# Batch 0 by token halves: a first G1 and G2 step before the second half is normalised

## Chip, cores, metric

One core of one Trainium2 chip. The metric is device time in microseconds, from repeated executions.

## The reference, cut to what matters

```python
def _attn_ref(x, state):                      # x: 8 batches, 8 heads, 512 tokens, 64; state: 32 slots
    scores = scale * x @ state^T ; a = softmax(scores)       # per token, over the 32 slots
    xread = a @ state
    ...                                                      # sread: the same from the state's side
    return concatenate([xread, sread], axis=2)
def _moe_ref(x, w_in, w_out):                 # 4352 rows, 512 -> 2048 -> 512
    h = x @ w_in ; g = h * sigmoid(h)
    return g @ w_out
```

The kernel folds `state @ w_in` into one matrix W1 per batch, so that h = a @ W1. For a batch, G1 computes h^T in 16 tiles of 128 features for all 512 tokens (two matmuls of 512 columns each, one SILU), and G2 multiplies each tile g by w_out, for four token tiles `tt` of 128 tokens. The tokens of a batch are also counted in chunks c0 to c3 of 128; SILU is h * sigmoid(h), and aT is the transposed a. Fillers are matmuls on zeros that keep TensorE busy.

## The kernel before: the parts concerned

```python
    for hg in range(2):                                   # x of batch 0, by halves of the heads
        nc.sync.dma_start(
            x_f[0][:, ds(4 * hg, 4), :, :],
            x[0, ds(4 * hg, 4)].rearrange("h (p c) d -> p h c d", p=128, c=4),
        )
    ...
    scores(0, 0)                     # 4 heads, all 512 tokens
    exps(0, 0)
    keep_busy(1, psH, "h1")          # filler matmuls on zeros
    pe_transpose_x(0, 1, 2, new_h, both)
    norm(0, 0)                       # GpSimd
    scores(0, 1, 2)
    exps(0, 1)
    norm(0, 1, ((nc.vector, 0, 4),), 2)
    w1_cols(0, [(0, 128)], (nc.scalar, nc.scalar))
    nc.scalar.activation(warm[:], busy[:, 0:1], func=SILU, bias=0.0)   # loads SILU's table
    load_w_in(1024) ...              # the later weight loads, on GpSimd
    keep_busy(3, psH, "h1")
    pss0 = w1_mms(0, [(128, 384)])
    keep_busy(2, psH, "h1")
    ...                              # 8 transposes of the normed scores, copies to aT
    upto(1)                          # G1 of tile 0 (g1_first)
    upto(2)                          # G1 of tile 1
    for ft in range(12):             # G2 with G1 ahead of it
        upto(min(ft + LEAD0[ft], ready))
        ...
```

The softmax here doesn't subtract the row's maximum and nothing guards it: scores larger than these inputs give would overflow.

## Time and profile before

| | before |
|---|---|
| median of 4 runs | 212.85 us (212.72 to 213.00) |
| span of the profiled run | 210.9 us |
| TensorE in the chain that ends last | 95% |
| first G2 product | 12.23 us |
| G1 of tile 5 | 17.73 us |
| last W1 product of batch 0 | 26.04 us |

The prediction shows the lines for these (it starts from 212.93 us, the median of the three runs that it had). The last three rows are the milestones for reading the change: after the last of them both kernels do the same work in the same order. How busy each engine is in the start-up, in stretches of 2 us (columns: stretch, its length, busy time of TensorE, its weight loads, VectorE, ScalarE, GpSimd, each with its instructions in brackets, then granted clock, DMA share, GB/s):

```profile
8.00:10.00 2.00, 1.80 (x28) 0.80 (x29) 1.90 (x7) 1.97 (x6) 0.93 (x1) 1.00 1.24 193
10.00:12.00 2.00, 1.96 (x23) 1.09 (x16) 1.91 (x7) 1.78 (x6) 2.00 (x4) 1.00 1.29 201
```

### The profile page before, as it was taken

The page shows a single profiled execution, that of the slowest core. Times are in us where ns is not written, and L with a number is a line of the kernel's source. Part 1 is how long each engine was busy: PE and PEld are TensorE (multiplying, and loading weights), DVE is VectorE, ACT ScalarE, POOL GpSimd, SP SyncE. Part 2 cuts the span into 40 slices and gives each one's busy share as a digit, 9 for nine tenths or more (in the row PEclk, how much of TensorE's full clock was granted, in tenths as well). Part 3 has the DMA queues.
Part 4 walks back from the last instruction along what each step waited for, and adds up shares of the span by engine and source line. Part 5 has one row for each costly group of instructions (what it writes and reads, how often), then busy time and mean ns, then how long its engine had stood idle before and what let it go on. Part 6 is the DMA issues. An engine that isn't in the chain of part 4 may idle for free.

```text
span 210.9 us, 3866 instructions
## 1 busy us (share of the span) xinstructions
PE 205.3 (97%) x1575; PEld 96.8 (46%) x1575; DVE 74.0 (35%) x146; ACT 139.2 (66%) x244; POOL 39.5 (19%) x62
## 2 busy tenths in 40 slices
PE   7899999999999999999999999999999999999993
PEld 2444354445444444444444544444444444466653
DVE  3851268567831336115211662043412306100011
ACT  3865677899577867697569855996775166644410
POOL 8681213704220402021201202000200000000000
PEclk9999999999999999999999999999999999999999
DMA  6999999995559475644925528115321111011112
GB/s 205 181 204 206 284 256 354 219 273 194 101 145 259 152 137 119 145 154 114 237 75 173 112 71 193 50 50 102 85 64 46 63 56 53 0 50 50 53 50 99
DMA packets 42929, 28.65 MB, mean 136 GB/s; under 512 B 28064, under 2 KB 37792, under 8 KB 42912
## 3 DMA queue, kind: packets, MB, share of 16 engines
q1 hardware_dynamic: 36720, 20.65, 37.7%
q0 software_dynamic: 5904, 7.64, 17.5%
q8 instruction: 12, 0.20, 0.4%
q10 hardware_dynamic: 288, 0.13, 0.2%
q14 instruction: 5, 0.04, 0.1%
HBM read 17.43 MB, written 8.91 MB: 125 GB/s over the span
## 4 chain that ended last, share of the span: by engine, by line
PE 95%; DMA 2%; DVE 1%; ACT 0%; issue 0%; DVEq 0%
PE o L566 51%; PE h L525 26%; PE ps_w L469 4%; PE h L546 3%; PE o_a L566 3%; DMA x_f<-in_x_dram 2%; PE o_part L588 2%; PE ps_sr L416 1%; PE ps_xt L253 1%; PE ps_sc L306 1%; PE ps_scT L332 1%; PE ps_busy L165 1%; PE ps_at L398 0%; PE h L507 0%; DVE W L159 0%; ACT xT L157 0%
## 5 line engine op out<-in xcount | busy, mean ns | idle before, releaser
L566 PE MATMUL o<-w_out_sb,g 128*128 128x512 bf16 x496 | 131.8, 379 | 0.0
L557 ACT ACTIVATE g<-h 128x512 bf16<-128x512 f32 (+1 forms) x143 | 81.2, 573 | 34.2 <-PE h L525 20.1
L566 PEld LDWEIGHTS <-g 128*128 128x128 bf16 x528 | 50.3, 98 | 59.0 <-issue 3.8
L525 PE MATMUL h<-aT,W 128*128 128x512 bf16 x254 | 74.5, 379 | 0.1
L159 DVE COPY o_sb<-o 128x512 f32<-128x512 f32 x15 | 10.4, 691 | 89.8 <-PE o L566 87.3
L525 PEld LDWEIGHTS <-W 128*128 128x128 bf16 x254 | 24.6, 98 | 30.5 <-issue 1.2
L159 DVE CAST W<-ps_w 128x512 bf16<-128x512 f32 (+2 forms) x36 | 22.2, 659 | 23.2 <-PE ps_w L469 23.2
L157 ACT ACTIVATE W<-ps_w 128x512 bf16<-128x512 f32 (+1 forms) x32 | 16.2, 562 | 11.1 <-PE ps_w L469 11.1
L159 POOL CAST x_nat<-x_f 128x512 bf16<-128x512 f32 x24 | 14.2, 631 | 35.9 <-DMA x_f<-in_x_dram 35.9
L157 ACT ACTIVATE o_sb<-o 128x512 f32<-128x512 f32 x16 | 9.5, 597 | 14.3 <-PE o L566 11.8
L362 POOL TENSOR_TENSOR an<-e,rcn 128x512 bf16<-128x512 bf16 x5 | 7.6, 1518 | 48.9 <-DVE rcn L360 39.3
L469 PE MATMUL ps_w<-w_in_sb,stT 64*32 64x512 bf16 (+2 forms) x264 | 10.1, 373 | 0.0
L566 PE MATMUL o_a<-w_out_sb,g 128*128 128x512 bf16 x32 | 10.0, 379 | 0.0
L546 PE MATMUL h<-xmT,w_in_sb 128*128 128x256 bf16 x64 | 9.6, 273 | 0.0
L546 PEld LDWEIGHTS <-w_in_sb 128*128 128x128 bf16 x64 | 6.3, 98 | 3.9
L165 PE MATMUL ps_busy<-busy 128*128 128x512 bf16 x16 | 5.8, 481 | 1.2 <-DVE warm L172 1.2
L359 DVE TENSOR_REDUCE rs<-e 128x32 f32<-128x1024 bf16 x5 | 6.1, 1211 | 2.1 <-DMA e<-eT 2.1
L346 ACT ACTIVATE eT<-ps_scT 128x512 bf16<-128x512 f32 x10 | 5.4, 594 | 1.6 <-PE ps_scT L332 1.6
L786 ACT ACT_TABLE_LOAD x5 | 6.4, 1283 | 0.1
L382 POOL TENSOR_TENSOR an<-exp_nat,rc 128x512 bf16<-128x512 bf16 x3 | 3.1, 1047 | 13.9 <-DMA x_f<-in_x_dram 8.7
L469 PEld LDWEIGHTS <-stT 64*32 64x32 bf16 x264 | 3.2, 90 | 5.2 <-issue 3.9
L768 ACT ACT_TABLE_LOAD x4 | 5.1, 1283 | 0.1
(76 smaller groups left out, 99.8 us busy)
## 6 DMA issues: line engine op xcount, KB each, us to landing
out_dram<-o_sb SPq DMA_DIRECT2D x33, 256.0 KB, 2.4
x_f<-in_x_dram SPq DMA_DIRECT2D x4, 1024.0 KB, 6.3
x_f<-in_x_dram POOLq DMA_DIRECT2D x2, 1024.0 KB, 12.6
w_in_sb<-in_moe_w_in_dram POOLq DMA_DIRECT2D x3, 512.0 KB, 10.2
x_f<-in_x_dram SPq DMA_DIRECT2D x2, 512.0 KB, 4.7
w_out_sb<-in_moe_w_out_dram POOLq DMA_DIRECT2D x4, 256.0 KB, 11.9
w_out_sb<-in_moe_w_out_dram POOLq DMA_DIRECT2D x2, 512.0 KB, 12.1
x_f<-in_x_dram POOLq DMA_DIRECT2D x2, 512.0 KB, 14.9
```

The source lines that it names most:

```text
L157: nc.scalar.activation(dst, src, func=COPY, bias=0.0)
L159: eng.tensor_copy(dst, src)
L165: nc.tensor.matmul(ps[:], busy[:, 0:128], busy[:], start=True, stop=True, skip_group_check=True)
L346: nc.scalar.activation(t[:, hg], scT_ps[hg][:], func=EXP, bias=0.0, scale=SCALE)
L359: nc.vector.tensor_reduce(rs[:], e2[b][:], axis=AX, op=ADD)
L362: eng.tensor_tensor(a[:, hg], e2[b][:, hg], rc[:, hg].to_broadcast([128, 4, 4, NS]), op=MULT)
L469: nc.tensor.matmul(pss[f, hg][ds(32 * s, 32), 0:n], stT[ds(r, 64), b, h // 2, s % 2, :], w_in_sb[ds(r, 64), h // 2, ds(f, n)], start=True, ...
L525: nc.tensor.matmul(h_ps[k][:], W1[b][:, hg, ds(128 * ft, 128)], aT[b][:, hg, :, :], start=(hg == 0), stop=(hg == 1), skip_group_check=True,)
L546: nc.tensor.matmul(ps[:, 0:256], w_in_sb[:, kt, ds(128 * ft, 128)], xmT[:, :, kt].rearrange("p t n b -> p t (n b)"), start=(kt == 0), stop ...
L557: nc.scalar.activation(g[:, 0:n], ps[:, 0:n], func=SILU, bias=0.0)
L566: nc.tensor.matmul(outs[tt][:], gt[b * NFT + ft][:, ds(128 * tt, 128)], w_out_sb[:, ft, :], start=(ft == 0), stop=(ft == NFT - 1), skip_gr ...
L786: nc.scalar.activation(warm[:], busy[:, 0:1], func=SILU, bias=0.0)
```

## The change

Intent: cut batch 0's attention by tokens instead of by heads. Chunks c0 and c1 (256 tokens, all heads) go through scores, softmax and transposes first; G1 of tiles 0 and 1 on these tokens and four G2 products then run while c2 and c3 are normalised. The core of the diff, with cuts:

```diff
-    for hg in range(2):
+    for half in range(2):
         nc.sync.dma_start(
-            x_f[0][:, ds(4 * hg, 4), :, :],
-            x[0, ds(4 * hg, 4)].rearrange("h (p c) d -> p h c d", p=128, c=4),
+            x_f[0][:, :, ds(2 * half, 2), :],
+            x[0].rearrange("h (p c) d -> p h c d", p=128, c=4)[:, :, ds(2 * half, 2), :],
         )
...
-    keep_busy(7, psH, "h1")
+    keep_busy(6, psH, "h1")
...
+    cast_x(0, nc.vector, 2, 1)
+    cast_x(0, nc.gpsimd, 3, 1)
+    load_w_out(4, 2)
+    load_w_out(6, 2)
+    sum0(0)
...
+    norm0(0, nc.vector)
+    norm0(1, nc.gpsimd)
...
+    turn_a0(0, in_bank("a3"))
+    turn_a0(1, in_bank("o0"))
+    pss0 = w1_mms(0, [(128, 384)], ...)
+    keep_busy(2, psA, "a0")
+    w1_out(0, [(128, 128)], (nc.vector, nc.vector), pss0)
+    g1_part(0, 0, new_h)                 # tile 0, first 256 tokens
+    keep_busy(1, psA, "a0")
+    g1_part(1, 0, new_h)
+    w1_out(0, [(128, 256)], (nc.scalar, nc.scalar), pss0, 128)
+    for c in (2, 3):
+        sum0(c)
+    nc.vector.reciprocal(rc0[:, 2:4], rs0[:, 2:4])
+    norm0(2, nc.vector)
+    norm0(3, nc.gpsimd)
+    load_w_in(1024) ...                  # the later weight loads
+    keep_busy(1, psA, "a0")
+    for ft in (0, 1):
+        for tt in (0, 1):
+            G2(0, tt, ft)
+    turn_a0(2, in_bank("a0"))
+    turn_a0(3, in_bank("a3"))
+    g1_part(2, 0, in_bank("a1"))
+    g1_part(3, 0, in_bank("a2"))
+    g1_part(0, 1)                        # tile 0, second 256 tokens
+    g1_part(1, 1)
...
+    for tt in (2, 3):
+        G2(0, tt, 0)
+    for tt in (2, 3):
+        G2(0, tt, 1)
+    pss = w1_mms(0, [(512, 512)])
```

More of the change, by code (lines that the diff above doesn't have):

```diff
@@ L195 @@
     load_w_in(512)
-    load_w_out(4, 4)
     both = (nc.vector, nc.scalar)
@@ L258, in pe_transpose_x @@
             copy(engs[u], xT[b][:, ds(m * u, m), ds(2 * hg, 2), :], ps[:])
-    cast_x(0, nc.vector, 0, 2, 0, 4)
-    cast_x(0, nc.scalar, 2, 2, 0, 4)
     for u in range(2):
@@ L269 @@
     new_o = lambda sh, dt, nm: psO.tile(sh, dt, tag=o_tags.pop(), name=nm)
-    cast_x(0, nc.scalar, 2, 2, 4, 4)
-    cast_x(0, nc.gpsimd, 0, 1, 4, 4)
-    pe_transpose_x(0, 0, 2, new_o, (nc.vector, nc.vector))
-    cast_x(0, nc.vector, 1, 1, 4, 4)
+    cast_x(0, nc.vector, 0, 1)
+    cast_x(0, nc.scalar, 1, 1)
     st_x = pers.tile([128, 8, B, 4, 2, 2], BF16)
@@ L496, with g1_part @@
     h_ps = {}
-    def g1_first():
-        g = gpool.tile([128, 512], BF16, tag="g", name="g")
-        gt[0] = g
-        pss = []
-        for i in range(2):
-            ps = psH.tile([128, 512], FP32, tag="h1", name="h1")
-            pss.append(ps)
-        for i in range(2):
-            for hg in range(2):
-                nc.tensor.matmul(
-                    pss[i][:, 0:256],
-                    W1[0][:, hg, 0:128],
-                    aT[0][:, hg, ds(2 * i, 2), :],
-                    start=(hg == 0),
-                    stop=(hg == 1),
-                    skip_group_check=True,
-                )
-        for i in range(2):
-            nc.scalar.activation(g[:, ds(256 * i, 256)], pss[i][:, 0:256], func=SILU, bias=0.0)
+    h0_ps = {}
+    def g1_part(k, half, new=None):
+        if half == 0:
+            h0_ps[k] = new([128, 512], FP32, "h1")
+            gt[k] = gpool.tile([128, 512], BF16, tag="g", name="g")
+        cols = ds(256 * half, 256)
+        for hg in range(2):
+            nc.tensor.matmul(
+                h0_ps[k][:, cols],
+                W1[0][:, hg, ds(128 * k, 128)],
+                aT[0][:, hg, ds(2 * half, 2), :],
+                start=(hg == 0),
+                stop=(hg == 1),
+                skip_group_check=True,
+            )
+        nc.scalar.activation(gt[k][:, cols], h0_ps[k][:, cols], func=SILU, bias=0.0)
     def g1_half(k, hg):
@@ L520, in g1_half @@
         if hg == 0:
-            if k == 1:
-                h_ps[k] = psA.tile([128, 512], FP32, tag="a1", name="h1")
-            else:
-                h_ps[k] = (bank if k in IN_BANKS else new_h)([128, 512], FP32, "h1")
+            h_ps[k] = (bank if k in IN_BANKS else new_h)([128, 512], FP32, "h1")
         nc.tensor.matmul(
@@ L536, in emit_G1 @@
         if b < B:
-            if k == 0:
-                g1_first()
-                return
             g1_half(k, 0)
@@ L609, with in_bank @@
     IN_BANKS = (4, 5)
-    new_o = lambda sh, dt, nm: psO.tile(sh, dt, tag=o_tags.pop(), name=nm)
+    def in_bank(tag):
+        return lambda sh, dt, nm: (psO if tag[0] == "o" else psA).tile(sh, dt, tag=tag, name=nm)
+    e0 = pers.tile([128, 4, H, NS], BF16)
+    an0 = pers.tile([128, 4, H, NS], BF16)
+    rs0 = pers.tile([128, 4, H, 1], FP32)
+    rc0 = pers.tile([128, 4, H, 1], FP32)
+    aT[0] = att.tile([128, 2, 4, 128], BF16, tag="aT", name="aT")
+    xT[0] = xtpool.tile([128, 4, 4, 128], BF16, tag="xT", name="xT0")
@@ new lines, with turn_x0, scores0 @@
+    for hg in range(2):
+        exp_nat[0, hg] = e0[:, :, ds(4 * hg, 4), :]
+    def turn_x0(c, new):
+        ps = new([128, 4, 128], BF16, "ps_xt")
+        for k in range(4):
+            nc.tensor.transpose(ps[:, k, :], x_nat[0][:, c, k, :], ident[:])
+        return ps
+    def scores0(c, new):
+        ps = new([128, H, NS], FP32, "ps_sc")
+        for k in range(4):
+            nc.tensor.matmul(
+                ps[:, ds(2 * k, 2), :],
+                xT[0][:, c, k, :],
+                stT[:, 0, k, :, :],
+                start=True,
+                stop=True,
+                skip_group_check=True,
+            )
+        nc.scalar.activation(e0[:, c], ps[:], func=EXP, bias=0.0, scale=SCALE)
@@ new lines, in sum0, with norm0, turn_a0 @@
+    def sum0(c):
+        nc.vector.tensor_reduce(rs0[:, c], e0[:, c], axis=AX, op=ADD)
+    def norm0(c, eng):
+        eng.tensor_tensor(
+            an0[:, c], e0[:, c], rc0[:, c].to_broadcast([128, H, NS]), op=MULT
+        )
+    def turn_a0(c, new):
+        ps = new([128, 2, 128], BF16, "ps_at")
+        for hg in range(2):
+            nc.tensor.transpose(ps[:, hg, :], an0[:, c, ds(4 * hg, 4), :], ident[:])
+        copy(nc.vector, aT[0][:, :, c, :], ps[:])
+    ps = turn_x0(0, in_bank("o0"))
@@ L611 @@
+    copy(nc.vector, xT[0][:, 0], ps[:])
+    ps = turn_x0(1, in_bank("o1"))
+    copy(nc.vector, xT[0][:, 1], ps[:])
     keep_busy(1, psH, "h1")
-    scores(0, 0)
-    exps(0, 0)
+    scores0(0, in_bank("a1"))
     keep_busy(1, psH, "h1")
-    pe_transpose_x(0, 1, 2, new_h, both)
-    norm(0, 0)
-    scores(0, 1, 2)
-    exps(0, 1)
-    norm(0, 1, ((nc.vector, 0, 4),), 2)
-    w1_cols(0, [(0, 128)], (nc.scalar, nc.scalar))
-    nc.scalar.activation(warm[:], busy[:, 0:1], func=SILU, bias=0.0)
+    scores0(1, in_bank("a2"))
@@ new lines @@
+    cast_x(0, nc.vector, 2, 1)
[3 more added lines that the diff above has]
+    sum0(0)
+    ps2 = turn_x0(2, in_bank("a3"))
+    ps3 = turn_x0(3, in_bank("o0"))
+    copy(nc.vector, xT[0][:, 2], ps2[:])
+    copy(nc.scalar, xT[0][:, 3], ps3[:])
+    sum0(1)
+    nc.vector.reciprocal(rc0[:, 0:2], rs0[:, 0:2])
+    norm0(0, nc.vector)
+    norm0(1, nc.gpsimd)
+    scores0(2, new_h)
+    w1_tags = ["a0", "o1"]
+    pss = w1_mms(0, [(0, 128)], lambda *a: in_bank(w1_tags.pop(0))(*a))
@@ new lines @@
+    scores0(3, new_h)
+    w1_out(0, [(0, 128)], (nc.vector, nc.vector), pss)
+    nc.scalar.activation(warm[:], busy[:, 0:1], func=SILU, bias=0.0)
+    turn_a0(0, in_bank("a3"))
+    turn_a0(1, in_bank("o0"))
+    w1_tags = ["a1", "a2"]
+    pss0 = w1_mms(0, [(128, 384)], lambda *a: in_bank(w1_tags.pop(0))(*a))
+    keep_busy(2, psA, "a0")
[4 more added lines that the diff above has]
+    w1_out(0, [(128, 256)], (nc.scalar, nc.scalar), pss0, 128)
@@ L632 @@
         ones_beside_x(i, nc.gpsimd)
-    keep_busy(3, psH, "h1")
-    banks[:] = ["a2", "a3"]
-    turn[0] = 0
-    pss0 = w1_mms(0, [(128, 384)])
-    keep_busy(2, psH, "h1")
-    for c in (0, 2):
-        ps_a = (psO, psA)[c // 2].tile(
-            [128, 2, 128], BF16, tag=("o1", "a0")[c // 2], name="ps_at"
-        )
-        at_mms(ps_a, 0, 0, c, 2)
-        copy(both[c // 2], aT[0][:, 0, ds(c, 2), :], ps_a[:])
-    for c in (0, 2):
-        ps_a = (psO, psA)[c == 0].tile(
-            [128, 2, 128], BF16, tag=("o0", "a1")[c == 0], name="ps_at"
-        )
-        at_mms(ps_a, 0, 1, c, 2)
-        copy(nc.vector, aT[0][:, 1, ds(c, 2), :], ps_a[:])
-    w1_out(0, [(128, 128)], both, pss0)
-    upto(1)
-    w1_out(0, [(128, 256)], (nc.vector, nc.vector), pss0, 128)
-    upto(2)
-    turn[0] = 0
-    W0 = {2: (512, 512), 6: (1024, 512), 10: (1536, 512)}
-    W1_AT = {2: 0, 6: 512}
-    LEAD0 = [2, 3, 2, 2, 2, 3, 2, 1, 3, 3, 2, 3]
-    T3 = {1: (0, 1), 2: (2,), 3: (3,), 4: (4,), 5: (5,), 6: (6,)}
-    ready = 4
-    for ft in range(12):
+    keep_busy(1, psA, "a0")
[8 more added lines that the diff above has]
+    g1_part(1, 1)
+    banks[:] = ["a3", "a2"]
+    turn[0] = 0
+    for ft, k in ((2, 2), (3, 3)):
+        for tt in (0, 1):
+            G2(0, tt, ft)
+        if k == 2:
+            place_one_state(1, transpose_one_state(st1_n), nc.vector)
+        g1_part(k, 1)
+    done[0] = 4
+    W0 = {6: (1024, 512), 10: (1536, 512)}
+    W1_AT = {6: 512}
+    LEAD0 = [2, 3, 2, 2, 2, 3, 2, 1, 3, 3, 2, 3]
+    T3 = {4: (4,), 5: (5,), 6: (6,)}
+    for tt in (2, 3):
[3 more added lines that the diff above has]
+    pss = w1_mms(0, [(512, 512)])
+    pss1 = w1_mms(1, [(0, 512)], new_h)
+    w1_out(0, [(512, 512)], both, pss)
+    w1_out(1, [(0, 512)], both, pss1)
+    for tt in (2, 3):
+        G2(0, tt, 2)
+    G2(0, 2, 3)
+    upto(5)
+    G2(0, 3, 3)
+    ready = 8
+    for ft in range(4, 12):
         upto(min(ft + LEAD0[ft], ready))
-        if ft == 1:
-            place_one_state(1, transpose_one_state(st1_n), nc.vector)
         if ft in W0:
```

## The prediction

> **What bounds the kernel now.** I read the page's busy shares and its chain first, then the timeline of the first 27 us, because the change touches only batch 0.
>
> ```profile
> PE 205.3 (97%) x1575; PEld 96.8 (46%) x1575; DVE 74.0 (35%) x146; ACT 139.2 (66%) x244; POOL 39.5 (19%) x62
> ...
> PE 95%; DMA 2%; DVE 1%; ACT 0%; issue 0%; DVEq 0%
> ```
>
> TensorE carries 95% of the chain that sets the end. So the span is a start-up, in which TensorE has little real work, plus a stream of matmuls at full speed. A change in batch 0 can only shorten the start-up; once the stream runs, its length is the count of matmuls. So the question is when the stream starts and with how much of it already done. The timeline of the start-up:
>
> ```profile
> 6.60 0.63 DVE L159 CAST x_rows<-x_f 128x256 bf16<-128x256 f32 x1
> 6.61 0.46 POOL L159 CAST x_rows<-x_f 128x256 bf16<-128x256 f32 x1
> ...
> 9.55 1.28 ACT L621 ACT_TABLE_LOAD   x1
> ...
> 9.70 0.11 PEld L469 LDWEIGHTS <-stT 64*32 64x32 bf16 x8 [0.48 <-DMA w_in_sb<-in_moe_w_in_dram]
> 9.70 0.36 PE L469 MATMUL ps_w<-w_in_sb,stT 64*32 64x384 bf16 x8
> ...
> 10.85 0.20 ACT L621 ACTIVATE warm<-busy 128x1 f32<-128x1 bf16 x1
> ...
> 11.70 0.66 ACT L516 ACTIVATE g<-h 128x256 bf16<-128x256 f32 x2 [0.21 <-PE h L507]
> 11.79 0.11 PEld L525 LDWEIGHTS <-W 128*128 128x128 bf16 x2 [0.19 <-DVE W L159]
> ...
> 12.23 0.59 PE L566 MATMUL o<-w_out_sb,g 128*128 128x512 bf16 x2
> ...
> 14.97 0.17 PEld L469 LDWEIGHTS <-stT 64*32 64x32 bf16 x16 [0.42 <-issue]
> ...
> 17.73 0.59 PE L525 MATMUL h<-aT,W 128*128 128x512 bf16 x2
> ```
>
> The second piece of w_in (128x384) lands at 9.70. SILU's table is in at 10.85. The first G2 product (o<-w_out) starts at 12.23 us, and the G1 step of tile 5 at 17.73. From 12.23 on TensorE is hardly idle; before it, 16 of its matmuls are fillers on zeros (ps_busy). Later the transfers come close to being a second bound:
>
> ```profile
> 26.04 0.41 PE L469 MATMUL ps_w<-w_in_sb,stT 64*32 64x512 bf16 x8
> ...
> 28.38 0.69 DVE L159 CAST x_rows<-x_f 128x1024 bf16<-128x1024 f32 x1 [0.58 <-DMA x_f<-in_x_dram]
> ```
>
> The last quarter of w_in, issued at 11.61 with at most 13.8 us to landing (longest of its five transfers), is there by about 25.4 and used at 26.04, so 0.6 us spare. VectorE waits for the second half of x of batch 1 until 28.38; its transposes run on TensorE at 30.12, while cast and hop allow about 29.1, so 1.0 us spare.
>
> **The Trainium skill.** (1) "TensorE: Matmul & The Clock Gate", "Wait — 56ns, not 53.3ns?": warm matmuls start N / 2.4 GHz + about 2.5 ns apart, 215.7 ns for 512 columns, hence 109 for 256. The trace agrees: ten G2 matmuls take 2.16 us in the chain, 216 ns each; the 379 ns shown for one includes its latency. (2) "DMA: Bandwidth & Descriptors", "Specifications": line rate needs transfers of at least 512 B. The new loads of x of batch 0 have runs of 2 x 64 x 4 = 512 B in place of 1024, right at that edge. The trace has both sizes, in the stretch from 2 to 5 us:
>
> ```profile
> q1 hardware_dynamic: 930, 0.94, 92.6%
> q10 hardware_dynamic: 101, 0.04, 5.3%
> ```
>
> 3 us x 16 engines x 0.926 / 930 is 48 ns per 1 KB packet; the state load (runs of 512 B) needs 48 us x 0.053 / 101 = 25 ns. So halving the runs should cost about 5%, 0.1 to 0.2 us on 1 MB. (3) "SBUF — State Buffer", "Who interferes with whom": a cast on VectorE and an op on GpSimd can lock each other out of a shared port pair. The trace agrees: in the two casts quoted, 256 elements took VectorE 0.63 us beside GpSimd, against 0.43 for 512 elements alone at 5.01. (4) "ScalarE: Activation LUTs", "What ACT_TABLE_LOAD costs": 1283 ns plus a drain of about 1380. The load agrees (1.28); here the next ACTIVATE follows 1.30 after its start, so I count no drain.
>
> **The change, part by part.** Tokens c0 and c1 come in the first x transfer, c2 and c3 in the second, each for all heads. I walked the new order on each engine with the durations above.
>
> *First half.* x lands at 4.91 in the chain before, say 5.0 now. VectorE casts c0 (0.43), ScalarE c1 (0.63); transposes and two xT copies on VectorE (0.42 each) end at about 6.7; scores by 7.0; exp of c0 and c1 (0.38 each) by 7.5.
>
> *Second half.* It lands at 6.43 before, say 6.55. GpSimd casts c3 beside VectorE's c2, both now 512 elements, the collision of (3): both done at about 7.4 (alone 7.05). Then TensorE turns c2 and c3, to 7.95; ScalarE copies c3 (0.60) to 8.65; the last two exps end at 9.45. ScalarE no longer copies the first W1 columns (0.44) but copies c3 here, so SILU's table loads at 9.45 to 10.75, and SILU can start at 10.9 to 11.0, against 11.05 before: a gain of 0.1.
>
> *Norm and W1 for the first half*, VectorE in its order: sum c0, xT c2, sum c1 (0.42 each), reciprocal 0.25, norm 0.4 (half of 0.70), to about 9.3; two W1 copies of 128x128 (0.28, overlapping a little) to 9.75; two aT copies (0.29) to 10.3; then W1 columns 128 to 255 to 10.8.
>
> *TensorE*: the 384-column W1 product still waits for its transfer, 9.70 to 9.8; it takes 0.36; two fillers to 10.55; G1 of tile 0 on 256 tokens to 10.77; filler; G1 of tile 1 at 11.0 to 11.2; filler to 11.4. SILU of tile 0 is 10.95 to 11.33. So the first G2 can start at about T0 = 11.42 at best, 0.8 earlier than 12.23. With a collision or a late weight I expect 11.4 to 11.9, mean 11.55.
>
> *But less is done by then.* Work on TensorE from the first G2 to G1 of tile 5, all 16 products of G2 tiles 0 to 3 between: before 16 x 0.216 (3.45) + G1 of tiles 2 to 4, 6 x 0.216 (1.29) + 16 W1 matmuls 0.58 + a transpose 0.07 = 5.39 (12.23 + 5.39 = 17.62; the trace says 17.73). After: 3.45 + twelve half-width G1 matmuls x 0.109 (1.31) + G1 of tile 4 0.43 + four transposes of the second half 0.26 + 0.58 + 0.07 = 6.10. So 0.71 us that stood before the stream now stands in it. Best case 11.42 + 6.10 = 17.52, a gain of 0.2; at the mean T0 of 11.55, 17.65, a gain of 0.1.
>
> *New waits inside the stream.* VectorE does the sums of c2, c3 (0.8), the reciprocal 0.25 and a norm 0.4 to 0.6 from 10.8 on, so to 12.2 to 12.5, while GpSimd norms c3. TensorE has four G2 products for that time and arrives at the transposes at 12.3; the two aT copies end at 13.1 to 13.4, and G1 of the second half, wanted at 13.1, needs both. I put 0 to 0.4 us of stall here, mean 0.2. ScalarE keeps up: six half SILUs of 0.38 and two copies of about 0.4 from 11.6 to 14.7, just ahead of their readers.
>
> *Moved transfers.* Loads of w_in from column 1024 on wait on GpSimd behind the norm of c3, issued near 12.4 instead of 10.07. The queue still has the second w_in quarter (used at 14.97) and 512 KB of w_out before it, so I expect no gap. Issuing w_out in two pieces costs about 0.75 us of GpSimd, off the path.
>
> Sum: 212.93 - 0.1 (earlier stream less work left over) + 0.2 (stall) = 213.0; the tuned filler counts suggest that the author found a schedule that meets its waits, so I shade this to 212.9.
>
> **Rivals.** (a) *A real gain of 0.6 to 1.2 us* (near 212.0): if the second half's work is hidden completely and VectorE and GpSimd do not collide. For it: the first half of x has been there since 4.91. Against it: w_in's second piece lands at 9.70 and the SILU table is in at 10.85 whatever the tokens do, so T0 has a floor near 11.4; and a gain above 0.6 to 1.0 meets the transfers of batch 1 and is capped there. (b) *A loss of 0.5 to 1.5 us* (near 213.9): 512-byte runs slower than the state load suggests (both x transfers and w_in behind them slip), or the VectorE chain of the second half missing its slot by more than 0.4, with TensorE stalled in order behind it. For it: VectorE has hardly a pause from 5 to 13 us. Against: 25 ns per packet. (c) *A starved queue*: if the late w_in issue leaves the DMA engines idle by a microsecond, the 0.6 spare at 26 us goes and the time is up to 213.5. Against: nearly 3 us of backlog.
>
> **Range and chances.** Predicted 212.9 us, range 212.1 to 213.8; chances 0.01 faster, 0.97 same, 0.02 slower. 2% is 4.3 us. Faster by that is ruled out, as the best T0 gains 0.8 of which 0.7 is given back; slower would need a stall three times rival (b). The range takes half of (a) and most of (b).
>
> **What would show it.** First G2 at 11.4 to 11.9 us; G1 of tile 5 at 17.5 to 18.0; table load near 9.45; w_in's second piece awaited at 9.7 to 9.9; stall on aT at most 0.4 us; the W1 piece at 26.04 and all after it moved by the same amount as G1 of tile 5. I am wrong if the first G2 comes before 11.2 or after 12.2, if the waits from 12 to 15 us sum to over 0.8, or if a transfer stops TensorE at 25 to 30 us.

## The result, and the profile after

The changed kernel takes 213.56 us (median of 4 runs, 213.46 to 213.61) against 212.85: 0.7 us longer. The ratio is 1.0032, 95% interval 1.0015 to 1.005, so the loss is small but real. Ratios here are the mean time of one kernel's fast runs over that of the other's in the same rounds, so not quite the ratio of the quoted medians.

The timeline of the changed kernel (start, length, engine, line, operation; in brackets the idle time before it and what ended that), in the order of the prediction's steps:

```profile
7.07 0.43 DVE L159 CAST x_rows<-x_f 128x512 bf16<-128x512 f32 x1 [0.20 <-DMA x_f<-in_x_dram]
7.10 0.86 POOL L159 CAST x_rows<-x_f 128x512 bf16<-128x512 f32 x1 [1.17 <-DMA x_f<-in_x_dram]
...
7.92 1.41 POOL L153 DMA_DIRECT2D w_out_sb<-in_moe_w_out_dram  x2
...
9.34 0.64 POOL L633 TENSOR_TENSOR an<-e,rc 128x256 bf16<-128x256 bf16 x1
...
9.83 1.28 ACT L669 ACT_TABLE_LOAD   x1
...
10.04 0.28 PE L640 MATMUL ps_at<-ident,an 128*128 128x128 bf16 x2 [0.21 <-POOL an L633]
...
10.25 0.36 PE L464 MATMUL ps_w<-w_in_sb,stT 64*32 64x384 bf16 x8
...
11.40 0.82 ACT L509 ACTIVATE g<-h 128x256 bf16<-128x256 f32 x2
...
11.85 1.03 PE L553 MATMUL o<-w_out_sb,g 128*128 128x512 bf16 x4
...
12.25 0.79 POOL L633 TENSOR_TENSOR an<-e,rc 128x256 bf16<-128x256 bf16 x1 [2.27 <-ACT g L509]
...
13.09 0.11 PEld L640 LDWEIGHTS <-an 128*128 128x128 bf16 x2 [0.27 <-POOL an L633]
...
18.38 0.59 PE L515 MATMUL h<-aT,W 128*128 128x512 bf16 x2
19.02 0.55 PEld L553 LDWEIGHTS <-g 128*128 128x128 bf16 x4 [0.53 <-ACT g L544]
...
26.91 0.41 PE L464 MATMUL ps_w<-w_in_sb,stT 64*32 64x512 bf16 x8
```

The stream does begin earlier: the first G2 product starts at 11.85 instead of 12.23. But G1 of tile 5 starts at 18.38 instead of 17.73, and the last W1 product at 26.91 instead of 26.04. The gain of 0.38 has turned into a loss of 0.87 within 15 us, and from there on both kernels need the same time (210.9 - 26.04 = 184.9 and 211.8 - 26.91 = 184.9 us), so nothing later in the kernel has a part in it. (The two profiled executions differ by 0.9 us, the medians by 0.7.)

The accounts, from starts in the two timelines:

| term | predicted | measured |
|---|---|---|
| first G2 earlier | -0.68 (mean T0 11.55) | -0.38 (11.85) |
| work left over for the stream | +0.71 | +0.71 (a count, 6.10 - 5.39) |
| waits from first G2 to G1 of tile 5 | +0.2 | +0.43 (18.38 - 11.85 - 6.10) |
| the same waits before | -0.11 | -0.11 (17.73 - 12.23 - 5.39) |
| waits from there to the last W1 product | 0 | +0.22 (8.53 - 8.31) |
| sum | +0.1 | +0.87 |

Of the waits, the idle time of the weight load at 13.09 shows one (TensorE wants the normed c3, which GpSimd finishes at 13.04), and that at 19.02 the other (SILU of tile 4, whose W1 columns were copied only just before). A weight load may wait while earlier matmuls still run, so its idle time is not all idle time of TensorE (0.53 us at 19.02, where the starts of the matmuls leave 0.21).

The loads of x also behave otherwise than foreseen. This is the DMA activity from 2 to 5 us in 40 slices, before, then after (tenths of busy time, averaged over the DMA engines); the line below the second is that of the queue of x in the changed kernel (packets, MB, share):

```profile
DMA  4954768879899999999999999999999999999999
```

```profile
DMA  7521000012036999999999999999999999999999
...
q1 hardware_dynamic: 1377, 0.70, 82.8%
```

In both kernels the first load of x is issued at 0.74 us. Before, x moves from about 2.2 us; after, the small state load moves at 2.0 to 2.3, and x begins at about 2.9 (a few packets from 2.5). A 512 B packet then takes 48 us x 0.828 / 1377 = 29 ns, not the 25 ns taken from the state load, against 48 ns for 1 KB before. So the first half is there at 5.15 (casts at 5.20) instead of 4.91, and the second at 7.05 instead of 6.43.

Finally the busy times after, for the same stretches as before:

```profile
8.00:10.00 2.00, 1.44 (x22) 0.79 (x22) 1.93 (x7) 1.42 (x4) 1.96 (x3) 1.00 1.27 205
10.00:12.00 2.00, 1.91 (x18) 1.04 (x20) 1.74 (x7) 1.87 (x4) 0.00 (x0) 1.00 1.29 199
```

VectorE is as full as before from 8 to 10 us (1.93 of 2 us); the change moved work off ScalarE and added some to GpSimd, which is full from 8 to 10 us and then waits. VectorE had little taken off it (from 4 to 12 us it is busy for 5.9 us, before for 6.1).

### The profile page after: what moved, and what is told of

Read it like the earlier page. It is cut to its first block, busy times and chain, and to the rows that moved or that the text cites. A ratio compares the mean times of both kernels' runs of the same rounds, so it can differ in the third digit from the quotient of the medians.

```text
span 211.8 us, 3854 instructions
## 1 busy us (share of the span) xinstructions
PE 203.9 (96%) x1554; PEld 96.9 (46%) x1579; DVE 74.7 (35%) x150; ACT 138.8 (66%) x245; POOL 41.8 (20%) x64
## 4 chain that ended last, share of the span: by engine, by line
PE 92%; DMA 3%; POOL 1%; issue 1%; DVE 1%; ACT 1%; SPq 0%
PE o L553 50%; PE h L515 25%; PE ps_w L464 4%; PE h L533 3%; PE o_a L553 3%; DMA x_f<-in_x_dram 3%; PE o_part L575 2%; PE ps_sr L411 1%; PE h L501 1%; PE ps_scT L327 1%; POOL an L633 1%; DVE W L159 0%; PE ps_sc L301 0%; PE ps_xt L252 0%; POOL x_rows L159 0%
## 5 line engine op out<-in xcount | busy, mean ns | idle before, releaser
L553 PE MATMUL o<-w_out_sb,g 128*128 128x512 bf16 x480 | 129.1, 379 | 1.3 <-issue 0.5
L544 ACT ACTIVATE g<-h 128x512 bf16<-128x512 f32 (+1 forms) x140 | 79.5, 573 | 33.0 <-PE h L515 18.9
L515 PE MATMUL h<-aT,W 128*128 128x512 bf16 x242 | 71.6, 379 | 0.1
L515 PEld LDWEIGHTS <-W 128*128 128x128 bf16 x248 | 24.0, 98 | 29.9 <-issue 1.2
L159 DVE CAST W<-ps_w 128x512 bf16<-128x512 f32 (+1 forms) x37 | 22.2, 641 | 22.9 <-PE ps_w L464 22.9
L159 POOL CAST x_nat<-x_f 128x512 bf16<-128x512 f32 x24 | 15.0, 668 | 34.9 <-DMA x_f<-in_x_dram 34.9
L553 PE MATMUL o_a<-w_out_sb,g 128*128 128x512 bf16 x30 | 9.4, 379 | 0.3 <-issue 0.2
L109 POOL DMA_DIRECT2D x_f<-in_x_dram x4 | 3.3, 842 | 9.4 <-DVE x_rows L159 7.0
```

What stands on the lines that cost most here:

```text
L159: eng.tensor_copy(dst, src)
L515: nc.tensor.matmul(h_ps[k][:], W1[b][:, hg, ds(128 * ft, 128)], aT[b][:, hg, :, :], start=(hg == 0), stop=(hg == 1), skip_group_check=True,)
L544: nc.scalar.activation(g[:, 0:n], ps[:, 0:n], func=SILU, bias=0.0)
L553: nc.tensor.matmul(outs[tt][:], gt[b * NFT + ft][:, ds(128 * tt, 128)], w_out_sb[:, ft, :], start=(ft == 0), stop=(ft == NFT - 1), skip_gr ...
```

## Two kinds of start

The experiments were timed with five rounds, and the runs of the changed kernel and its variants fall into groups, some 0.4 to 0.7 us or more apart. Where a longer one was profiled (e1, e2, e12), TensorE is slow up to 9 to 10 us. Here are the eight transposes of x, first in the changed kernel's profile (213.61 us), then in that of the first experiment (214.25 us):

```profile
5.68 0.62 PE L613 MATMUL ps_xt<-ident,x_rows 128*128 128x128 bf16 x8 [0.43 <-DVE x_rows L159]
```

```profile
5.71 1.04 PE L613 MATMUL ps_xt<-ident,x_rows 128*128 128x128 bf16 x8 [0.46 <-DVE x_rows L159]
```

The instructions are the same and take 1.04 us instead of 0.62, a filler 0.63 instead of 0.38. The column of the granted clock reads 1.00 in both, so only the durations show it. It is the slow pace of the start that lasts longer: in every profile the first fillers follow each other at 0.43 us, in a quick stretch at 0.22; the changed kernel is quick by 5.7 us in its own profile, e1 only after 9 us. A second kind is in e10's profile (215.83): its transposes take 0.62, but the clock column reads 0.70 from 10 to 12 us and 0.50 from 12 to 14. And in e12's and e10's profiles the first half of x also came later (casts at 5.89 and 5.42 instead of 5.20). So a long run need not have one cause. Across all executions, the changed kernel had 3 long ones in 10 (214.15, 214.21, 215.12), the kernel before none so far off among 37 (212.71 to 213.44 without a clear gap). The change leaves TensorE less to do early: from 4 to 12 us it is busy 6.46 us, before 6.91 (sums over the four stretches of 2 us), and it has two fillers fewer. That this causes the long starts is possible, not shown: no run changed the fillers alone. Below, "short runs" are the lower group of a kernel, "long" the rest; which run belongs where I read from its time, and only for the profiled ones from durations. In short runs the changed kernel is at 213.46 to 213.61 on both of its chips.

## The experiments

Twelve kernels in three calls, each beside the kernel before on its chip (medians 212.81, 212.87 and 213.06).

### e1: the two w_out loads behind the norm of c1

```diff
-    load_w_out(4, 2)
-    load_w_out(6, 2)
     ...
     norm0(1, nc.gpsimd)
+    load_w_out(4, 2)
+    load_w_out(6, 2)
```

> The changed kernel, with the two w_out loads issued on GpSimd behind the norm of token chunk c1 instead of ahead of it. My theory: GpSimd's two issues (7.92 to 9.33 us) hold back that norm (9.34, its sums were ready at about 9.05), so the transposes of c1 (10.04) and the 384-column W1 product (10.25) come about 0.3 us late. Theory expects them at about 9.75 and 9.95, the first G2 only 0.05 to 0.1 us earlier (the SILU table is in at 11.33 anyway), the VectorE chain of the second half 0.3 us earlier, and a time 0.1 to 0.3 us below the changed kernel (213.3 to 213.4 beside 212.85 for before). Rival, that only the late x transfer paces this stretch: first G2 at 11.83 again and no change of time (213.5).

Measured: short runs 213.41, 213.54, 213.57; long 214.10, 214.11, 214.25 (median of all 213.84, ratio 1.0041). The short ones are 0.70 above before, as with the changed kernel (0.66 to 0.7). No gain: GpSimd's two issues from 7.92 to 9.33 don't set the end by themselves. Its profile fell in a long start, so its times within the start-up can't be compared. It does show a detail: there GpSimd's cast issued first (7.07, 0.61 us) and VectorE's at 7.12 took 0.83, while in the changed kernel VectorE came first and GpSimd's took 0.86. Whoever starts first holds up the other, as the Trainium skill has it ("SBUF — State Buffer", "Who interferes with whom"). Here the first keeps its usual time and the second takes 0.40 us longer where it is VectorE, and 0.25 us longer where it is GpSimd, so less than the page's full block for the 0.40 us in which they overlap; only in the kernel before, where they start 0.01 us apart (6.60 and 6.61), is the one shown first the slow one.

### e2: the norm of c3 on VectorE

```diff
-    norm0(3, nc.gpsimd)
+    norm0(3, nc.vector)
```

> The changed kernel, with the norm of chunk c3 on VectorE instead of GpSimd. Theory, that the GpSimd norm (0.79 us beside VectorE's own, ends 13.04) is what TensorE waits for at 13.09: norm ends near 12.9, wait falls by 0.1 to 0.2 us, time 0.1 to 0.2 us below the changed kernel (213.3 to 213.5). Rival, that VectorE is as full as GpSimd is late: the aT copies slip by what the norm gains, time 213.5 to 213.7.

Measured: short 213.45 and 213.50, long 213.90 to 213.99 (median 213.90, ratio 1.0042). The short runs are 0.05 us under the changed kernel's, less than their scatter. The rival holds or the gain is below 0.1; which of the two is not shown, as its profile fell in a long start.

### e3: no normalisation of the second half (wrong result)

```diff
-    for c in (2, 3):
-        sum0(c)
-    nc.vector.reciprocal(rc0[:, 2:4], rs0[:, 2:4])
-    norm0(2, nc.vector)
-    norm0(3, nc.gpsimd)
     ...                                     # in turn_a0:
-    nc.tensor.transpose(ps[:, hg, :], an0[:, c, ds(4 * hg, 4), :], ident[:])
+    nc.tensor.transpose(ps[:, hg, :], (an0 if c < 2 else e0)[:, c, ds(4 * hg, 4), :], ident[:])
```

> Wrong result on purpose: the changed kernel without sums, reciprocal and norm of the second half (its transposes read the exponentials). Theory, that the second half's normalisation does not fit beside the four G2 products and stalls TensorE: the 0.4 us of idle time between 12.2 and 18.4 us goes, time 0.3 to 0.5 us below the changed kernel (213.0 to 213.2). Rival, that the waits there are for SILU and for W1 copies, or that the loss is the work left over: at most 0.1 us less (213.4 to 213.5).

Measured: short 213.25 to 213.41 (five), one long 214.16. That is 0.2 us less than the changed kernel, about half of what I expected. In its trace the first G2 is at 11.85 as before and G1 of tile 5 at 18.20 instead of 18.38. So the second half's normalisation costs 0.2 us, and with none of it the kernel would still lose 0.5: hiding it perfectly could not make the change pay.

### e4: the kernel before with the new x loads alone

```diff
-    for hg in range(2):
+    for half in range(2):
         nc.sync.dma_start(
-            x_f[0][:, ds(4 * hg, 4), :, :],
-            x[0, ds(4 * hg, 4)].rearrange("h (p c) d -> p h c d", p=128, c=4),
+            x_f[0][:, :, ds(2 * half, 2), :],
+            x[0].rearrange("h (p c) d -> p h c d", p=128, c=4)[:, :, ds(2 * half, 2), :],
         )
```

> The kernel before with nothing changed but the two x loads of batch 0, cut by token halves (runs of 512 B) as in the change. Theory, that the 512 B runs start later and move slower: the halves land at about 5.15 and 7.05 us as in the changed kernel, against 4.91 and 6.43; here most casts need the second, so time 0.6 to 1.3 us above before (213.5 to 214.2). Rival, that the late landing has another cause in the changed kernel (order of the state load, other traffic): landings at 4.9 and 6.4, time up by less than 0.5 us.

Measured: 217.32 us (216.73 to 217.54), ratio 1.0205 (1.0191 to 1.0219, so "unclear" at the 2% mark, though longer by far more than the noise). The landings are as the theory says: casts wait for them until 5.09 and 6.95 us, so the late second half belongs to the loads, not to the rest of the change. The time went up by 4.5 us instead of 0.6 to 1.3, and the profiled run (216.73) has a reason in the clock column:

```profile
6.00:8.00 2.00, 0.55 (x9) 0.34 (x7) 0.42 (x1) 1.00 (x3) 1.18 (x3) 1.00 1.46 192
8.00:10.00 2.00, 1.93 (x19) 1.37 (x16) 0.79 (x3) 1.12 (x2) 0.00 (x0) 0.52 1.27 205
10.00:12.00 2.00, 1.71 (x20) 0.85 (x19) 1.76 (x5) 1.53 (x5) 0.71 (x1) 0.50 1.29 200
```

TensorE had only 0.55 us to do in 2 us, and was then granted half its clock for nearly 7 us (about 8.1 to 14.9). Here the second half of x came 0.5 us later (6.95 against 6.43) and the time went up by 3.9 us. The other three runs were longer still (217.26 to 217.54) with a listed mean clock of 0.998; they were not profiled, so what they lost their time to is open.

### e5: the changed kernel again

> The changed kernel again, as the yardstick on this chip. Two of its variants and the kernel before showed two groups of times some 0.4 to 0.6 us apart, and the profiles of the longer ones showed matmuls of twice the length from about 6 to 10 us. Expected: most runs 213.4 to 213.6, and a few near 214.1 with the same long matmuls; 0.7 us above before.

Measured: 213.49, 213.52, 213.59, and 214.15, 214.21, 215.12; ratio 1.0056. The two groups are there; one run in six even lost 1.6 us more. So in use the change costs 0.7 us at best and about 1.2 on average (0.0056 x 212.8).

### e6: four x loads of 256 KB instead of two

```diff
     for half in range(2):
-        nc.sync.dma_start(x_f[0][:, :, ds(2 * half, 2), :], ...)
+        for hg in range(2):
+            nc.sync.dma_start(x_f[0][:, ds(4 * hg, 4), ds(2 * half, 2), :], ...)
```

> The changed kernel with each token half of x of batch 0 loaded by two transfers of 4 heads (256 KB) instead of one of 8 heads, same 512 B runs. In the changed kernel no x moves until about 2.85 us, in the kernel before until 2.25. Theory, that a transfer starts only when all its runs have been prepared, and that twice the runs cost the 0.6 us: x starts at 2.2 to 2.4, first half lands at 4.6 to 4.9 instead of 5.15, second at 6.4 to 6.7 instead of 7.05, the SILU table is in 0.3 to 0.5 us earlier, time 0.2 to 0.5 us below the changed kernel. Rival, that short runs move slowly whatever the start: landings at 5.1 and 7.0, no change of time.

Measured: 218.66 us (218.24 to 219.94), ratio 1.0279. The start came as the theory has it: x moves from 2.2 us, at full rate from 2.6, and the first half is cast at 4.98. But the second half landed only at 10.25:

```profile
10.31 0.43 DVE L159 CAST x_rows<-x_f 128x512 bf16<-128x512 f32 x1 [3.62 <-DMA x_f<-in_x_dram]
```

The packets by queue show how: from 4 us on, packets of GpSimd's queue, whose first loads are w_in's (first seen at 4.0 to 4.5 us), share the DMA engines with those of x, and x's rate falls from 0.17 MB per 0.5 us to 0.08, then 0.02. With two large loads, the first packets of that queue came when x was nearly through (6.0 to 6.5). So the theory holds for the start: in these kernels a load of 1024 runs starts 0.6 to 0.7 us later than one of 512, whether those are of 512 B or of 1 KB. That the finer cut is what let the other traffic in is the likely reading, from this one run. TensorE then idled from 7 to 10.8 us and was granted half its clock from about 11.3 to 18.2 us, which can make up the rest.

### e7: the four early G2 products behind the second half

```diff
-    keep_busy(1, psA, "a0")
-    for ft in (0, 1):
-        for tt in (0, 1):
-            G2(0, tt, ft)
     turn_a0(2, in_bank("a0"))
     ...
     g1_part(1, 1)
+    for ft in (0, 1):
+        for tt in (0, 1):
+            G2(0, tt, ft)
```

> The changed kernel with the four early G2 products (and the filler ahead of them) moved behind the transposes and G1 steps of the second half, so nothing overlaps its normalisation. Theory: the four products (4 x 0.216 = 0.86 us) fill a wait that VectorE and GpSimd set, so they come on top: time 0.6 to 0.9 us above the changed kernel (214.2 to 214.4). Rival, that the overlap is worth nothing because TensorE is the bound there anyway: within 0.2 us of the changed kernel.

Measured: 214.27 to 214.42 in the four shortest runs, 0.8 us above the changed kernel's short runs; median 214.39, ratio 1.0082. The overlap that the change was made for works and is worth about 0.8 us, nearly all of the 0.86. What loses is what it takes to get there.

### e8: the changed kernel with x by halves of the heads

The x loads of the kernel before, in the changed kernel (the reverse of e4's diff).

> The changed kernel with x of batch 0 loaded by halves of the heads as before (runs of 1 KB): every cast then needs both transfers. Theory: they land at 4.9 and 6.4 to 6.5, so the first half of the tokens starts 1.25 us later and the second 0.6 us earlier than in the changed kernel; as the second half and the SILU table set the pace from 7 us on, the first G2 is later by 0.3 to 1.0 us, time 213.7 to 214.5. If the late second half alone sets the pace, the time falls to 213.1 to 213.4.

Measured: 214.99 to 215.34, median 215.29, ratio 1.0113. Casts wait until 6.52, as expected, and the first G2 comes at 13.63, 1.8 us later, where I had 0.3 to 1.0; its matmuls from 7 to 9.3 us are of the long kind (eight transposes 1.04 us), which is part of the 1.8. So the token loads are the right ones for this order, late as they land.

### e9: casts of c2 and c3 that need no second load (wrong result)

```diff
-    cast_x(0, nc.vector, 2, 1)
-    cast_x(0, nc.gpsimd, 3, 1)
+    cast_early(nc.vector, 2)        # writes c2 from x_f's c0
+    cast_early(nc.gpsimd, 3)        # writes c3 from x_f's c1
```

> Wrong result on purpose: the changed kernel with the casts of chunks c2 and c3 reading c0 and c1, so that nothing waits for the second x transfer (it still runs). Theory, that its landing at 7.05 sets the chain cast, transpose, copy, exp, SILU table: the table load starts at 9.1 to 9.3 instead of 9.83, the first G2 comes at 11.4 to 11.6 instead of 11.85, time 0.25 to 0.5 us below the changed kernel (213.0 to 213.3 in the runs with a warm start). Rival, that VectorE's queue sets the first G2 whatever lands when: 11.75 or later, time within 0.1.

Measured: shortest runs 213.49, 213.53, 213.64 (median of six 213.76, ratio 1.0046). Against its own before runs (median 213.06) that is 0.5 us, against the changed kernel's short runs nothing; before was 0.2 us slower in this call, so 0.2 us either way stays open by time. The trace decides:

```profile
9.55 1.28 ACT L676 ACT_TABLE_LOAD   x1
...
9.96 0.28 PE L640 MATMUL ps_at<-ident,an 128*128 128x128 bf16 x2 [0.19 <-POOL an L633]
...
10.18 0.36 PE L464 MATMUL ps_w<-w_in_sb,stT 64*32 64x384 bf16 x8
...
11.78 1.03 PE L553 MATMUL o<-w_out_sb,g 128*128 128x512 bf16 x4
```

The table load moves up by 0.28 us, the first G2 by 0.07; and in e5's profile of the changed kernel as it is, it is at 11.78 too, so even the 0.07 is scatter. The theory falls: the late second half, which the chain of waits of the changed kernel names as its first link, isn't what holds the first G2 by itself. The edit moved more than the casts: GpSimd's w_out issues also came earlier (6.49 to 7.90 instead of 7.92 to 9.33), so its norm of c1 no longer stood behind them and started at 9.14, 0.17 us after VectorE's reciprocal, instead of at 9.34; but it took 0.77 us instead of 0.64 and ended at 9.91 against 9.98. So its transposes and the W1 product come when they came. What did not move is VectorE's queue: in both runs its sum of c1 starts at 8.3 and the reciprocal at 8.7 to 8.8.

### e10: W1 products one G2 product earlier

```diff
-    for tt in (2, 3):
-        G2(0, tt, 1)
+    G2(0, 2, 1)
     pss = w1_mms(0, [(512, 512)])
+    G2(0, 3, 1)
```

> The changed kernel with the W1 products of batch 0's second quarter one G2 product earlier (between the third and fourth of the token tiles 2 and 3). In the changed kernel the chain W1 product, copy, G1 of tile 4, SILU leaves TensorE idle for about 0.2 us at 19.0. Theory: that wait shrinks, time 0.1 to 0.2 us below the changed kernel (213.3 to 213.4 warm). Rival: the bank that the product needs is free only at 16.2, so it moves by little and the time stays (213.5).

Measured: short runs 213.75 to 213.85 beside before at 213.06, so 0.74 above, against 0.66 to 0.7 for the changed kernel; two long ones at 215.8 and 215.9. No gain, as the rival expects; its reason, the bank, isn't checked, as the profile is of a long run.

### e11: the kernel before with two G2 products moved into a later wait

```diff
-    T3 = {..., 6: (6,)}
+    T3 = {..., 6: (6,), 10: (7, 8)}
     ...
-    G2(0, 3, 7)
     scores(1, 0, new=new_h)
-    for ft in range(8, 12):
+    for ft in range(9, 12):
```

> The kernel before with two G2 products of token tile 3 (ft 7 and 8) moved up behind those of ft 10, where its trace shows TensorE idle for 0.45 us (26.8 to 27.3) while VectorE and ScalarE copy the last W1 columns. Not part of the change; both kernels have this wait. Theory: 0.43 us of work moves into it, time 0.3 to 0.45 us below before (212.4 to 212.5). Rival, that the two products were the filler of a later wait (transposes and scores of batch 1 at 31 us) or that x of batch 1 lands too late: less than 0.15 us gained.

Measured: 213.03 against 213.06, ratio 1.0002 (0.999 to 1.0014): nothing. The wait near 27 us is filled, and these came in its place:

```profile
31.81 0.29 PEld L306 LDWEIGHTS <-xT 128*128 128x128 bf16 x8 [0.40 <-DVE xT L159]
...
34.85 0.23 PEld L398 LDWEIGHTS <-an 128*128 128x128 bf16 x4 [0.54 <-POOL an L382]
```

The two products had been the filler of the scores and transposes of batch 1. In the kernel before, the weight load for those transposes waited 0.19 us for that norm; here 0.54.

### e12: the edits together

The diffs of e2 and e10 in the changed kernel, and e11's edit.

> The changed kernel with the edits that lost nothing put together: norm of c3 on VectorE, W1 products one G2 earlier, and the two G2 products moved behind ft 10. Theory: gains add to 0.5 to 0.7 us against the changed kernel, 212.8 to 213.1 in warm runs: about level with before, and 0.3 to 0.6 us above the kernel before with the last edit alone, because the 0.7 us of work left over stay. Rival, that x of batch 1 lands too late for an earlier stream: 213.2 or more.

Measured: 213.79 to 215.92, median 214.26, ratio 1.0065. Small edits that each gained nothing gain nothing together, and no version of mine beats the kernel before.

## Why the prediction was right, and where it was off

The measured 213.56 lies in the range (212.1 to 213.8), near its upper end, and "within 2%" was right. The centre was not: 212.9 stands for no change, and the kernel became 0.7 us longer, clear of noise. Point by point:

- *TensorE bounds, and only the start-up can change.* Right: from the last W1 product on both kernels take 184.9 us.
- *An earlier first G2, with 0.71 us of work left over.* The mechanism was right and is the main reason for the loss: the start gains 0.38 and the stream has 0.71 more to do. e7 shows that the overlap itself is real (0.8 us).
- *T0 at 11.42 to 11.9, mean 11.55.* It came at 11.85, in the range, 0.3 above the mean. The step that failed is "the 384-column W1 product still waits for its transfer, 9.70 to 9.8". It starts at 10.25 and waits for no transfer: in TensorE's order it stands behind the transposes of c1, which wait for GpSimd's norm of c1 until 9.99. I had walked each engine and left those transposes out of TensorE's order. Nor was the issue of w_out off the path: the norm of c1 starts at 9.34, when the two issues end (9.33), though the reciprocal is done at 9.02. What would bring T0 forward is not settled: the load order on GpSimd (e1) gave no gain in time, and e9, which moved SILU's table by 0.28 and the start of that norm by 0.20 at once, none either. VectorE's queue, which feeds the norm, stayed as it was. So did the fillers: from 10.25 to 11.85 TensorE runs without a pause, and four fillers of 0.216 are 0.86 of these 1.60 us. Two of them stand before G1 of tile 0 (10.98), whose last copy of aT is there at 10.65. In the changed kernel SILU's table, ready at 11.33 with its warm-up, would leave little of that to gain (SILU of tile 0 starts at 11.40); in e9, with the table ready at 11.05, up to 0.28 us. No run took fillers out there, so this rival stands untested.
- *Second half lands at 6.55, casts done at 7.4, table load at 9.45.* Mis-sized: 7.05, 7.96 and 9.83. Halved runs cost 0.6 us on the second landing, not 0.1 to 0.2; a start 0.6 to 0.7 us later, which I had not thought of, is of that size. The packet times were no good guide to the rate, as packets overlap (shares above 100% of the engines' time). But e9 shows that this error hardly mattered.
- *A stall of 0 to 0.4, mean 0.2, from the second half's norm.* It was 0.43 in all up to tile 5; e3 puts the norm's own part at 0.2.
- *No further waits.* Wrong by 0.22: SILU of tile 4 at 19.02, after W1 copies that stand closer to their use than before. So two signs missed: G1 of tile 5 came at 18.38, not at 17.5 to 18.0, and the W1 product at 26.04 moved by 0.87, not by the same 0.65.
- *No starved queue, no transfer in the way from 25 to 30 us.* Right: the last W1 product has no wait for a transfer, though w_in's third quarter was issued at 12.98 instead of 10.07.
- *Shaded from 213.0 to 212.9* because the filler counts look tuned: the wrong way.
- *Not foreseen:* longer starts in 3 runs of 10.

So rival (b) came nearest in size, but not by its causes alone: late x and a late VectorE chain account for little by e9 and e3. That the number fell within the range owes something to the range's width: it took in most of rival (b).

## What to carry to other kernels

When TensorE is the bound, count what is already done when the stream starts, not only when it starts: an earlier first product that leaves 0.7 us of other matmuls for later needs 0.7 us of earlier start to break even. Look also at the engine that prepares the step: here VectorE was full from 8 to 10 us before and after, so the split gave it no room (what that cost is not shown). And a pause in the start-up must be kept short: in e4 the second half of x came 0.5 us later and the time rose by 3.9 us or more, in e6 the second half came 3.2 us later than in the changed kernel and the time rose by 5.1; in both profiles a stretch of half clock of about 7 us follows the pause.

## What the Trainium skill lacked or had wrong

- "DMA: Bandwidth & Descriptors", "Specifications" gives about 0.6 us from issue to first byte for loads of this kind. Here x begins to move about 1.5 us after the issue with 512 runs in a load, 2.1 us with 1024, and 1.5 in e6 with 512 again (full rate there after 1.9). No page that I read says that the start grows with the number of runs.
- The same table calls 512 B enough for line rate. Measured from 3 to 5 us, where hardly anything but x moves: 329 GB/s in runs of 512 B against 373 GB/s in runs of 1 KB, 12% less (means of four stretches of 0.5 us).
- "ScalarE: Activation LUTs", "What ACT_TABLE_LOAD costs" adds a drain of about 1380 ns to the load's 1283. In the kernel before the next ACTIVATE started 1.30 us after the load's start; no drain is seen.
- "TensorE: Matmul & The Clock Gate", Part 1, describes the throttled start and warns that the clock events of a trace are not always reliable; the runs give a case with numbers: the clock column reads 1.00 while matmuls take 0.63 us instead of 0.38 (e1), so durations have to be looked at.
